# A filter in the frequency domain: first and last groups take another route through the engines

## The chip, the cores and the metric

The kernel runs on one core of one Trainium2 chip. A core has five engines with a queue of instructions each: TensorE (matmuls; PE in the profile), VectorE (DVE), ScalarE (ACT), GpSimd (POOL) and SyncE (SP), which here only issues transfers. The metric is the device time of one execution in microseconds; the median of several runs is compared.

## The reference, cut to what matters

Four layers alternate, each with a residual: layer A filters a layer-normed input in the two-dimensional frequency domain, and layer B is an attention over segments with a memory.

```python
def _A_ref(x, w_r, w_i):          # x: (1, 2048, 640)
    X = rfft2(x.astype(float32))  # 2048 x 321 complex
    X = X * (w_r + 1j * w_i)
    return irfft2(X, s=(2048, 640)).astype(bfloat16)

x = x + _A_ref(_layernorm(x), A_w_r, A_w_i)
x = x + _B_ref(_layernorm(x), ...)
x = x + _A_ref(_layernorm(x), A_w_r, A_w_i)
x = x + _B_ref(_layernorm(x), ...)
```

Only layer A is touched by the change; it occurs twice.

## The kernel before, in words

A layer A has three stages. The first multiplies the input by sine and cosine tables along part of the token axis and leaves `YT`. The second, `spectrum`, is what the change is about. The third, `tokens`, transforms back to rows (`psg`, L541, is its first matmul for each of 16 sets of rows; `psy`, L551 to L555, its second), adds the residual and computes the layer norm of layer B.

`spectrum` works through eight groups of frequencies, numbered j = 1, 2, 3, 4, 5, 6, 7, 0 in that order (`SEQ`). For each group it runs these steps:

- `along_d` (L420): two times ten matmuls of 321 columns transform the model axis, with cosines (o = 0, called ac) and with sines (o = 1, called db). ScalarE copies db to a buffer in SBUF, `dbs` (L428).
- `combine` (L432): VectorE writes the sum and the difference of ac and db as four bf16 rows, `P[j]` (L439, L440). Group 0 needs neither: its ac and db are only cast, one by VectorE (L437), one by ScalarE (L436).
- `across` (L442): for each of the two signs `sg`, four matmuls of `P[j]` against constants `K` finish the transform in two PSUM banks, `X`.
- `filt` (L453): for each sign, VectorE multiplies `X` by the real and by the imaginary filter values (L456): four products per group.
- `products` (L458): VectorE subtracts the products (L462), GpSimd adds them (L467; VectorE does that for groups 7 and 0), and GpSimd writes sum and difference of the two results as bf16, `sd[j]` (L469, L470). Before its addition GpSimd copies one element (`turn`, L466), which makes it wait for the subtraction. Group 0 needs no sum and difference.
- `back` (L472): for each of three chunks of the 321 columns (128, 128, 65), four matmuls of 256 columns (L488; L483 for group 0) begin the inverse transform in a PSUM bank, which ScalarE copies to `UT` (L490; VectorE for one chunk of group 0).

The order on TensorE, ScalarE, VectorE and GpSimd inside `spectrum` is the order of the text (`manual_schedule`, L493): the loop from L495 takes, for each i, the two transforms of group i, the steps across for group i - 1 and the way back of group i - 3, interleaved by hand. Every engine takes its own instructions strictly in that order. The PSUM pool of the stage has three pairs of banks with the tag `pg`, taken in turn by ac, db, X and one chunk of group 0, and two single banks with the tag `pu` for the other chunks of `back`. A step that takes a pair must wait until the reader of its last user is done. `SyncE` issues the filter rows of a later group after `products` (`load_w`, L514), and, gated by small ScalarE copies, the tables of the stage that follows and constants of layer B.

`BStart.begin` (L1480) reserves the transposed input of layer B; `BStart.memory` (L1501) clears the gaps in it with four memsets on GpSimd, during `tokens`.

Of the kernel before, what the change touches and what calls it, by code (L numbers as in the profile page):

```python
# [13 lines left out]
ALU = mybir.AluOpType  # L14
# [6 lines left out]
NF = 321  # L21
# [7 lines left out]
def _dft_tables():  # L29
# [22 lines left out]
    f = np.arange(321.0)  # L52
# [25 lines left out]
    for part in range(2):  # L78
        P = (1j if part else 1) * np.exp(1j * ps)
        for c in range(2):  # L80
            for k in range(8):
# [8 lines left out]
                for e, z in enumerate((se, de)):  # L90
                    M[c, part, e, :, k, :, q], M[c, part, e, :, k, :, r] = z.real, z.imag
    M = M.reshape(2, 2, 2, 128, 128)
    cK = np.stack([-kc, -ks, kc, ks] + [m for c in range(2) for m in (Kf[c].real, Kf[c].imag, -Kf[c].real)]
                  + [M[c, part, e] for c in range(2) for part in range(2) for e in range(2)], 1)
# [97 lines left out]
class LayerA:  # L192
# [8 lines left out]
    def tables(self, gate=None, mirror=True):  # L201
        nc, cd = self.tc.nc, self.g["cd"]
        s5 = self.ar.get("S5", f"{self.lname}tab")
        self.Fd = s5.bf(5, 2, NF)
        self.K = s5.bf(18, 128)
        self.Wm = s5.bf(2, 7 * NF)
        self.wts = [s5.bf(2, NF) for _ in range(3)]
        self.W = {}
        self.load_w(0)
        nc.sync.dma_start(out=self.Fd, in_=cd["cFd"])  # L210
        nc.sync.dma_start(out=self.K, in_=cd["cK"])
        self.load_w(1)
        self.load_w(2)
        for i in range(2 if mirror else 0):
            if gate is not None:
                _gate(nc, self.Wm[0:1, i, 0:1], gate)
            self.load_mirror(i)
# [175 lines left out]

    def spectrum(self, late_loads=()):
        tc, g, YT, Fd, K = self.tc, self.g, self.YT, self.Fd, self.K
# [5 lines left out]
        dbs = s1.f32(2, NF)  # L401
# [18 lines left out]
        def along_d(j, o):  # L420
            ab[j, o] = ps = pp.tile([128, 2, 512], FP32, name=f"ab{o}", tag="pg", bufs=3)
            for ch in range(5):
                for c in range(2):
                    nc.tensor.matmul(ps[:, 1 - c if o else c, 0:NF], lhsT=YT[:, ch, 2 * j + c, :, :].rearrange("p s k -> p (s k)"), rhs=Fd[:, ch, o, :],
                                     start=(ch == 0), stop=(ch == 4))
            if o == 1 and j:
                ab[j, o] = dbs
                nc.scalar.copy(out=dbs, in_=ps[:, :, 0:NF])  # L428

        pos = {j: p for p, j in enumerate(self.SEQ)}  # L430

        def combine(j):  # L432
            P[j] = quads[pos[j] % 2]
            ac, db = ab[j, 0], ab[j, 1]
            if j == 0:
                nc.scalar.copy(out=P[j][:, 2:4, :], in_=db[:, :, 0:NF])  # L436
                nc.vector.tensor_copy(out=P[j][:, 0:2, :], in_=ac[:, :, 0:NF])  # L437
                return
            nc.vector.tensor_tensor(out=P[j][:, 0:2, :], in0=ac[:, :, 0:NF], in1=db, op=ALU.add)  # L439
            nc.vector.tensor_tensor(out=P[j][:, 2:4, :], in0=ac[:, :, 0:NF], in1=db, op=ALU.subtract)  # L440

        def across(j, sg):  # L442
            X[j, sg] = x = pp.tile([128, 2, 512], FP32, name="X", tag="pg", bufs=3)
            if j == 0:
                a, b = (0, 3) if sg == 0 else (1, 2)
                k = 4 + 3 * sg
                ops = [(0, k, a), (0, k + 1, b), (1, k + 1, a), (1, k + 2, b)]
            else:
                ops = [(0, 2, 0), (0, 3, 3), (1, 2, 3), (1, 1, 0)] if sg == 0 else [(0, 2, 2), (0, 3, 1), (1, 0, 1), (1, 3, 2)]
            for i, (o, k, p) in enumerate(ops):  # L450
                nc.tensor.matmul(x[:, o, 0:NF], lhsT=K[:, k, :], rhs=P[j][:, p, :], start=(i % 2 == 0), stop=(i % 2 == 1))

        def filt(j, sg):  # L453
            x = X[j, sg]
            for t, xv, i in ((ts[pos[j] % 2][0], x[:, :, 0:NF], 0), (ts[pos[j] % 2][1], x[:, ::-1, 0:NF], 1)):
                nc.vector.tensor_tensor(out=t[:, sg, :, :], in0=xv, in1=W[j, sg][:, i, :].unsqueeze(1).to_broadcast([128, 2, NF]), op=ALU.mult)  # L456

        def products(j):  # L458
            sd[j] = quads[2 + pos[j] % 3]
            t1, t2 = ts[pos[j] % 2]  # L460
            a = sd[j].rearrange("p (c s) f -> p c s f", c=2) if j == 0 else acs[pos[j] % 2]
            nc.vector.tensor_tensor(out=a[:, 0, :, :], in0=t1[:, :, 0, :], in1=t2[:, :, 0, :], op=ALU.subtract)  # L462
            add = nc.vector
            if pos[j] < 6:
                add = nc.gpsimd
                add.tensor_copy(out=turn, in_=a[0:1, 0, 0, 0:1])  # L466
            add.tensor_tensor(out=a[:, 1, :, :], in0=t1[:, :, 1, :], in1=t2[:, :, 1, :], op=ALU.add)  # L467
            if j:
                nc.gpsimd.tensor_tensor(out=sd[j][:, 0:2, :], in0=a[:, :, 0, :], in1=a[:, :, 1, :], op=ALU.add)  # L469
                nc.gpsimd.tensor_tensor(out=sd[j][:, 2:4, :], in0=a[:, :, 0, :], in1=a[:, :, 1, :], op=ALU.subtract)  # L470

        def back(j, chunks):  # L472
            for ch in chunks:
                f0, f1 = CH[ch]
                m = f1 - f0
                if j == 0 and ch == 1:
                    psu = pp.tile([128, 2, 512], FP32, name="psu0", tag="pg", bufs=3)[:, 0, :].rearrange("p (e c k) -> p e c k", e=2, c=2)
                else:
                    psu = pp.tile([128, 2, 2, 128], FP32, name="psu2", tag="pu", bufs=2)
                if j == 0:  # L480
                    for c in range(2):
                        for part in range(2):
                            nc.tensor.matmul(psu[0:m, :, c, :], lhsT=sd[j][:, 2 * part + c, f0:f1], rhs=K[:, 10 + 4 * c + 2 * part:12 + 4 * c + 2 * part, :],  # L483
                                             start=(part == 0), stop=(part == 1))
                else:
                    for e, ops in enumerate((((0, 256), (3, 128)), ((1, 0), (2, 128)))):
                        for i, (o, k) in enumerate(ops):
                            nc.tensor.matmul(psu[0:m, e, :, :], lhsT=sd[j][:, o, f0:f1], rhs=Kf[:, k:k + 256], start=(i == 0), stop=(i == 1))  # L488
                for e in range(2):
                    (nc.vector.tensor_copy if j == 0 and ch == 1 else nc.scalar.copy)(out=UT[0:m, ch, e, :, j * 16:j * 16 + 16].rearrange("p s (c k) -> p s c k", c=2),  # L490
                                                                                in_=psu[0:m, e, :, :].rearrange("p c (s k) -> p s c k", k=8))

        with tc.manual_schedule(engines={nc.tensor.engine, nc.scalar.engine, nc.vector.engine, nc.gpsimd.engine}):  # L493
            rest = None
            for i in range(8 + 3):  # L495
                j, last, done = [self.SEQ[k] if 0 <= k < 8 else None for k in (i, i - 1, i - 3)]
                if j is not None:
                    along_d(j, 1)
                if rest is not None:
                    back(rest, (2,))  # L500
                    for _ in range(2):
                        if late:
                            late.pop(0)(UT[0:1, 0, 0, 0, rest * 16:rest * 16 + 1])
                if last is not None:
                    across(last, 0)
                    filt(last, 0)
                if j is not None:
                    along_d(j, 0)
                    combine(j)
                if last is not None:  # L510
                    across(last, 1)
                    filt(last, 1)
                    products(last)
                    if i + 2 < 8:  # L514
                        self.load_w(i + 2)
                rest = done
                if done is not None:
                    back(done, (0, 1))
            back(rest, (2,))
            for f in late:  # L520
                f(UT[0:1, 0, 0, 0, 112:113])

    def tokens(self, x_dst, xn_dst, handoff=None):
# [8 lines left out]
        pp = self.pp  # L532
        if handoff is not None:
            handoff.begin()

        def spectrum_d(s0):
# [935 lines left out]
class BStart:  # L1472
# [7 lines left out]
    def begin(self):  # L1480
        self.hT = self.ar.get("S2", f"{self.lname}hT").bf(5, self.st.NK + 12)

    def wv_piece(self, i):
# [17 lines left out]
    def memory(self, pp):  # L1501
        nc = self.tc.nc
        for a, b in self.st.hgap:
            nc.gpsimd.memset(self.hT[:, :, a:b], 0.0)
        psm = pp.tile([128, 5, 128], BF16, name="psm0", tag="pu", bufs=2)
# [170 lines left out]
def kernel(  # L1676
# [26 lines left out]
    a1.cold(A_x[0])  # L1703
    a1.spectrum(late_consts(tc, g))
    a1.tokens(x1[:], n1[:], b1)
    layer_B(tc, g, ar, b1, x1[:], None, f1, a2)
    a2.spectrum()
    a2.tokens(x3[:], n3[:], b2)
# [49 lines left out]
```

## Time and profile before

| what | time |
|---|---|
| median of 5 runs | 1566.17 us (1565.74 to 1567.28) |
| the profiled execution's own time | 1567.24 us |
| its span, from the first to the last instruction | 1565.40 us |
| first spectrum stage, first L424 to first L541 | 26.50 to 76.79 us |
| second spectrum stage, first L424 to first L541 | 795.43 to 845.41 us |
| mean granted clock of TensorE | 0.997 of full speed |

Instruction rows give start, duration, engine, line, operation, output and inputs with their shapes, a count where several are merged, and in brackets the idle time of the engine before the row with what ended it. Durations overlap their successors by a little[...]; the step from one start to the next is the rate.

### The profile page before, as it was taken

Reading aid. Unit: us, or ns where it says so; the run is one execution under the profiler, and the core shown is the slowest. Engines: PE = TensorE matmul, PEld = TensorE weight load, DVE = VectorE, ACT = ScalarE, POOL = GpSimd, SP = SyncE. Lnnn points to the kernel's source line nnn. Section 1 sums busy time; section 2 is a strip of 40 time slices with the busy share of each in tenths; the row PEclk is TensorE's granted clock in tenths of the full one; section 3 lists DMA queues with packets and bytes.
Section 4 is the critical chain, followed back from the end, with each engine's and each line's share of the span. In section 5 each row is a group of like instructions: output and inputs, shape, how many; then the busy total and the mean of one; then the engine's idle time right before and its main releaser. Section 6 shows DMA issues by size and latency. Waiting matters only on the chain. (4 is left out here: it accounts for less than half of the span.)

```text
span 1565.4 us, 36413 instructions
## 1 busy us (share of the span) xinstructions
PE 1531.0 (98%) x14418; PEld 1073.5 (69%) x14419; DVE 816.9 (52%) x2438; ACT 768.9 (49%) x2245; POOL 238.5 (15%) x329
## 2 busy tenths in 40 slices
PE   7999999999999999999999999999999999999998
PEld 6676666666666666677766766666666666667775
DVE  7872545565456555633377635565456555553111
ACT  4484565555555565511126655556555565562000
POOL 3620021111111121100034101111111121110000
PEclk9999999999999999999999999999999999999999
DMA  4681334334443443636114614434443435427242
GB/s 170 206 298 44 115 132 157 137 124 149 148 141 137 141 131 149 197 104 179 51 48 140 199 38 155 137 126 146 150 140 137 146 126 176 126 99 229 68 128 64
DMA packets 159764, 214.79 MB, mean 137 GB/s; under 512 B 7136, under 2 KB 133096, under 8 KB 151648
## 3 DMA queue, kind: packets, MB, share of 16 engines
q1 hardware_dynamic: 159008, 210.08, 40.9%
q8 instruction: 114, 1.87, 0.5%
q0 software_dynamic: 576, 2.30, 0.4%
q14 instruction: 66, 0.54, 0.1%
HBM read 167.26 MB, written 45.10 MB: 136 GB/s over the span
## 5 line engine op out<-in xcount | busy, mean ns | idle before, releaser
L1087 PEld LDWEIGHTS <-bB_S 128*128 128x128 bf16 x3180 | 261.3, 97 | 179.8 <-issue 0.6
L1146 DVE CAST bB_S<-psk 128x495 bf16<-128x495 f32 (+3 forms) x320 | 191.6, 599 | 277.0 <-PE psk L1087 272.3
L1429 PE MATMUL psx<-Wo_sb,bB_S 128*128 128x320 bf16 x2048 | 287.7, 299 | 0.1
L1166 ACT ACTIVATE bB_S<-pss 128x269 bf16<-128x269 f32 (+5 forms) x576 | 208.9, 387 | 138.5 <-PE pss L1163 138.2
L1429 PEld LDWEIGHTS <-bB_S 128*128 128x128 bf16 x2048 | 196.7, 98 | 74.7 <-DVE bB_S L1250 0.7
L1131 ACT ACTIVATE bB_S<-psq 128x96 bf16<-128x96 f32 x300 | 152.1, 507 | 173.3 <-PE psq L1087 173.3
L1206 POOL TENSOR_TENSOR bB_S<-bB_S,bB_S 128x535 f32<-128x535 f32 x90 | 111.6, 1253 | 819.7 <-DVE bB_S L1198 762.3
L1250 DVE TENSOR_TENSOR bB_S<-pso,bB_S 128x480 bf16<-128x480 f32 (+1 forms) x320 | 192.7, 603 | 74.0 <-DMA bB_S<-Rd 52.0
L1167 DVE TENSOR_TENSOR bB_S<-bB_S,maskf 128x269 bf16<-128x269 bf16 (+5 forms) x576 | 158.8, 289 | 112.4 <-ACT bB_S L1166 112.4
L1155 ACT CAST bB_S<-psv 128x512 bf16<-128x512 f32 (+1 forms) x288 | 162.4, 564 | 80.9 <-PE psv L1153 80.9
L1153 PE MATMUL psv<-bB_S,B1hT_S 128*128 128x256 bf16 x1360 | 168.8, 273 | 0.0
L1153 PE MATMUL psv<-bB_S,B2hT_S 128*128 128x256 bf16 x1360 | 168.8, 273 | 0.0
L1087 PE MATMUL psk<-B1hT_S,bB_S 128*128 128x495 bf16 (+3 forms) x800 | 164.3, 343 | 0.2 <-ACT bB_S L1108 0.2
L1087 PE MATMUL psk<-B2hT_S,bB_S 128*128 128x495 bf16 (+3 forms) x800 | 164.3, 343 | 0.2 <-ACT bB_S L1108 0.2
L1087 PE MATMUL psq<-B1hT_S,bB_S 128*128 128x495 bf16 (+5 forms) x780 | 156.0, 337 | 0.0
L1087 PE MATMUL psq<-B2hT_S,bB_S 128*128 128x495 bf16 (+5 forms) x780 | 156.0, 337 | 0.0
L1153 PEld LDWEIGHTS <-B1hT_S 128*128 128x128 bf16 x1360 | 129.9, 98 | 24.3
L1153 PEld LDWEIGHTS <-B2hT_S 128*128 128x128 bf16 x1360 | 129.9, 98 | 24.3
L1163 PE MATMUL pss<-bB_S 128*128 128x132 bf16 (+8 forms) x1152 | 137.7, 219 | 0.0
L1163 PEld LDWEIGHTS <-bB_S 128*128 128x128 bf16 x1152 | 95.5, 98 | 55.3
L1236 PE MATMUL pso<-bB_S,bB_S 128*128 128x132 bf16 (+8 forms) x1152 | 118.7, 219 | 2.1 <-DVE oTmf L1253 1.4
L1236 PEld LDWEIGHTS <-bB_S 128*128 128x128 bf16 x1152 | 89.1, 98 | 34.7 <-DVE oTmf L1253 2.8
(283 smaller groups left out, 1427.9 us busy)
## 6 DMA issues: line engine op xcount, KB each, us to landing
bB_S<-Rd SPq DMA_DIRECT2D x62, 1070.0 KB
oTx_d<-bB_S SPq DMA_DIRECT2D x60, 512.0 KB
bB_S<-oTx_d SPq DMA_DIRECT2D x46, 512.0 KB
bB_S<-in_B_Wq_dram SPq DMA_DIRECT2D x32, 320.0 KB
bB_S<-in_B_Wk_dram SPq DMA_DIRECT2D x32, 320.0 KB
bB_S<-in_B_Wv_dram SPq DMA_DIRECT2D x32, 320.0 KB
Wo_sb<-in_B_Wo_dram SPq DMA_DIRECT2D x4, 1280.0 KB
B1wv_S<-in_B_Wv_dram SPq DMA_DIRECT2D x10, 512.0 KB
```

The costliest lines, as they stand in the source:

```text
L1087: nc.tensor.matmul(ps, lhsT=w[:, ch, hh * 128:(hh + 1) * 128], rhs=src[:, ch, lo:hi], start=(ch == 0), stop=(ch == 4))
L1131: nc.scalar.mul(out=qv[:, :, 0:SEG], in_=x_view(ps, o, n)[:, :, 1:SW], mul=scale)
L1146: nc.vector.tensor_copy(out=KTs[h % 2][:, lo:hi], in_=ps[:, 0:hi - lo])
L1153: nc.tensor.matmul(ps[:, i * 256:(i + 1) * 256], lhsT=hT[:, ch, st.hcol((t + i) * 128):st.hcol((t + i) * 128) + 128], rhs=w["Wv"][:, ch, : ...
L1155: nc.scalar.copy(out=V[:, t:t + n, :].rearrange("p a b -> p (a b)"), in_=ps[:, 0:n * 256])
L1163: nc.tensor.matmul(ps[:, off - o0:off - o0 + hi - lo], lhsT=KT[:, t * 128:(t + 1) * 128], rhs=QT[:, lo:hi], start=True, stop=True)
L1166: nc.scalar.activation(out=E[:, 0:n], in_=ps[:, 0:n], func=ACTF.Exp)
L1167: nc.vector.tensor_tensor(out=P[:, o0:o0 + n], in0=E[:, 0:n], in1=bs.mask[:, o0:o0 + n], op=ALU.mult)
L1206: nc.gpsimd.tensor_tensor(out=acc, in0=acc, in1=part, op=ALU.add)
L1236: nc.tensor.matmul(pso[:, lo - q0:hi - q0], lhsT=V[:, t, (h % 2) * 128:(h % 2 + 1) * 128], rhs=P[:, off:off + hi - lo], start=(i == 0), st ...
L1250: nc.vector.tensor_tensor(out=oT.rearrange("p (r s j) -> p r s j", r=16, j=2)[:, :, s0:s0 + ns, :], in0=byclass(po), in1=rx, op=ALU.mult)
L1429: self.tc.nc.tensor.matmul(ps[:, 0:320], lhsT=lhs(h, k // 2), rhs=self.g["Wo_sb"][:, h, c0:c0 + 320], start=(h == 0), stop=(h == H - 1))
```

## The change

- The first group's ac and db (j = 1) go to `P[j]` as bf16 by two ScalarE copies, without sum and difference. `across` then takes eight matmuls for each sign instead of four, with the signs in the constants; `K` gets one more matrix (-kc, now 19). Group 0's cast of ac moves from VectorE to ScalarE.
- For groups 6 and 7 (`SPLIT`) `products` writes the difference (VectorE) and the sum (GpSimd) of the filter products straight to `sd[j]` as bf16. `back` takes eight matmuls per chunk instead of four, four on each half, so that no sum and difference on GpSimd is needed. Group 7's halves are ordered so that its two first chunks use the first half before the second.
- The first filter product of group 0 goes to GpSimd, after a ScalarE copy of X from PSUM to `dbs`.
- Group 0's subtraction and addition are each cut in two pieces of 128 and 193 columns.
- The last chunk of groups 6 and 7 takes a spare pair of banks (`pg`); the chunks of one call get their banks first and are copied out after all of them have been multiplied.
- The order is written out anew: group 1 goes across for both signs before group 2 is transformed; group 7's `products` come after group 0's first sign.
- The four memsets move from `memory` to `begin`, which is now called at the end of `spectrum`.

```diff
-    cK = np.stack([-kc, -ks, kc, ks] + [m for c in range(2) for m in (Kf[c].real, Kf[c].imag, -Kf[c].real)]
+    cK = np.stack([-kc, -ks, kc, ks, -kc] + [m for c in range(2) for m in (Kf[c].real, Kf[c].imag, -Kf[c].real)]
...
-            if o == 1 and j:
+            if o == 1:
+                P[j] = quads[pos[j] % 2]
                 ab[j, o] = dbs
-                nc.scalar.copy(out=dbs, in_=ps[:, :, 0:NF])
+                nc.scalar.copy(out=P[j][:, 2:4, :] if j in RAW else dbs, in_=ps[:, :, 0:NF])
...
+        Q = self.SEQ
+        RAW, SPLIT = (Q[0], 0), Q[5:7]
...
-            if j == 0:
-                nc.scalar.copy(out=P[j][:, 2:4, :], in_=db[:, :, 0:NF])
-                nc.vector.tensor_copy(out=P[j][:, 0:2, :], in_=ac[:, :, 0:NF])
+            if j in RAW:
+                nc.scalar.copy(out=P[j][:, 0:2, :], in_=ac[:, :, 0:NF])
                 return
...
+            elif j in RAW:
+                ops = ([(0, 2, 2), (0, 1, 3), (1, 1, 2), (1, 0, 3), (0, 2, 0), (0, 3, 1), (1, 2, 1), (1, 1, 0)] if sg == 0 else
+                       [(0, 0, 2), (0, 3, 3), (1, 1, 2), (1, 0, 3), (0, 2, 0), (0, 3, 1), (1, 0, 1), (1, 3, 0)])
...
+                mul = nc.vector
+                if j == 0 and sg == 0 and i == 0:
+                    nc.scalar.copy(out=dbs, in_=xv)
+                    mul, xv = nc.gpsimd, dbs
+                mul.tensor_tensor(out=t[:, sg, :, :], in0=xv, in1=W[j, sg][:, i, :].unsqueeze(1).to_broadcast([128, 2, NF]), op=ALU.mult)
...
+            a = sd[j].rearrange("p (c s) f -> p c s f", c=2) if j == 0 or j in SPLIT else acs[pos[j] % 2]
+            for f0, f1 in ((0, 128), (128, NF)) if j == 0 else ((0, NF),):
+                nc.vector.tensor_tensor(out=a[:, 0, :, f0:f1], in0=t1[:, :, 0, f0:f1], in1=t2[:, :, 0, f0:f1], op=ALU.subtract)
+                add = nc.vector
+                if j:
+                    add = nc.gpsimd
+                    add.tensor_copy(out=turn, in_=a[0:1, 0, 0, 0:1])
+                add.tensor_tensor(out=a[:, 1, :, f0:f1], in0=t1[:, :, 1, f0:f1], in1=t2[:, :, 1, f0:f1], op=ALU.add)
+            if j and j not in SPLIT:
...
+                if ch == (1 if j == 0 else 2) and pos[j] > 4:
...
+            for ch, m, psu in outs:
+                inverse(j, ch, m, psu, 0)
+                if j == Q[5]:
+                    inverse(j, ch, m, psu, 1)
+            for ch, m, psu in outs if j == Q[6] else ():
+                inverse(j, ch, m, psu, 1)
...
+            elif j in SPLIT:
+                for e, ks in enumerate(((256, 256), (128, 384)) if part == 0 else ((128, 384), (0, 0))):
+                    for s, k in enumerate(ks):
+                        nc.tensor.matmul(psu[0:m, e, :, :], lhsT=sd[j][:, 2 * part + s, f0:f1], rhs=Kf[:, k:k + 256], start=(part + e + s == 0),
+                                         stop=(part + s == 2), skip_group_check=True)
...
+            def gate(p, sg):
+                across(Q[p], sg)
+                filt(Q[p], sg)
+                if sg and p != 6:
+                    products(Q[p])
+                    if p < 5:
+                        self.load_w(p + 3)
...
+            first_half(0)
+            second_half(0)
+            gate(0, 0)
+            gate(0, 1)
+            first_half(1)
+            second_half(1)
+            for p in range(2, 8):
+                first_half(p)
+                if p >= 4:
+                    rest(p - 4)
+                gate(p - 1, 0)
+                second_half(p)
+                gate(p - 1, 1)
+                if p >= 3:
+                    back(Q[p - 3], (0, 1))
+            gate(7, 0)
+            products(Q[6])
+            rest(4)
+            gate(7, 1)
+            for p in range(5, 8):
+                back(Q[p], (0, 1))
+                rest(p)
...
+            if handoff is not None:
+                handoff.begin()
```

Here `first_half` is `along_d` with sines, `second_half` is `along_d` with cosines and `combine`, and `rest` is `back` for chunk 2 with the gated loads.

## The prediction

> **What bounds the kernel now.** I read the page first, then its 40 slices, then stretches of the time line by stage.
>
> ```profile
> PE 1531.0 (98%) x14418; PEld 1073.5 (69%) x14419; DVE 816.9 (52%) x2438; ACT 768.9 (49%) x2245; POOL 238.5 (15%) x329
> ```
>
> TensorE (PE) is busy nearly everywhere, so only stretches in which it waits can give time back without taking matmuls away. The table of busy time by stretch shows where: the two spectrum stages.
>
> ```profile
> 24.80:74.00 49.20, 43.68 (x329) 30.60 (x326) 44.46 (x60) 18.74 (x58) 28.74 (x30) 0.99 0.51 167
> 110.00:795.20 685.20, 681.55 (x6499) 476.16 (x6499) 345.76 (x1112) 337.90 (x1021) 79.33 (x78) 1.00 0.40 131
> 795.20:843.00 47.80, 42.90 (x306) 29.83 (x307) 43.78 (x62) 17.34 (x51) 28.73 (x30) 0.98 0.19 54
> ```
>
> The columns are the stretch, its length, the busy time of PE, PE's weight loads, VectorE (DVE), ScalarE (ACT) and GpSimd (POOL), PE's clock, the DMA share, GB/s. In a spectrum stage VectorE is busy for 44 of 48 us, as long as PE. The middle groups repeat every 5.33 us, with PE back to back and VectorE full. The tail is different (time line of PE; the bracket is PE's idle time and its releaser):
>
> ```profile
> 835.41 1.26 PE L451 MATMUL X<-A2tmp_S,A2tab_S 128*128 128x321 bf16 x8
> 836.51 0.27 PE L488 MATMUL psu<-A2tab_S,A2tmp_S 128*128 128x256 bf16 x1
> 837.09 0.94 PE L488 MATMUL psu<-A2tab_S,A2tmp_S 128*128 128x256 bf16 x7 [0.31 <-POOL A2tmp_S L470]
> 838.33 0.60 PE L488 MATMUL psu<-A2tab_S,A2tmp_S 128*65 128x256 bf16 x4 [0.30 <-ACT A2UT_S L490]
> 839.91 0.28 PE L488 MATMUL psu<-A2tab_S,A2tmp_S 128*128 128x256 bf16 x1 [0.99 <-POOL A2tmp_S L469]
> 841.19 2.56 PE L488 MATMUL psu<-A2tab_S,A2tmp_S 128*128 128x256 bf16 x11 [0.99 <-POOL A2tmp_S L470]
> 843.59 1.99 PE L483 MATMUL psu<-A2tab_S,A2tmp_S 128*128 128x256 bf16 x12
> 845.41 2.04 PE L541 MATMUL psg<-A2gt_S,A2UT_S 128*128 128x321 bf16 x12
> ```
>
> From 836.5 on PE waits for GpSimd's sums and differences (L469, L470), which wait for VectorE. And the waiting slows PE itself; by single microseconds the columns are length, PE busy, clock, DMA share, GB/s:
>
> ```profile
> 840.00:841.00 1.00, 0.20 (x1) 1.00 0.00 0
> 841.00:842.00 1.00, 0.81 (x4) 0.62 0.00 0
> 842.00:843.00 1.00, 1.00 (x7) 0.50 0.00 0
> 843.00:844.00 1.00, 1.00 (x7) 0.50 0.00 0
> 844.00:845.00 1.00, 1.00 (x8) 0.67 0.00 0
> ```
>
> The clock halves for 3.3 us after the stretch with little work. The first stage shows the same at 73.4 to 76.7. VectorE and GpSimd in the tail:
>
> ```profile
> 835.71 1.32 POOL L470 TENSOR_TENSOR A2tmp_S<-A2gt_S 128x642 bf16<-128x642 f32 x1
> 836.38 1.34 DVE L462 TENSOR_TENSOR A2gt_S<-A2tmp_S 128x642 f32<-128x642 f32 x1
> 837.64 0.82 DVE L467 TENSOR_TENSOR A2gt_S<-A2tmp_S 128x642 f32<-128x642 f32 x1
> 838.54 1.32 POOL L469 TENSOR_TENSOR A2tmp_S<-A2gt_S 128x642 bf16<-128x642 f32 x1 [1.08 <-DVE A2gt_S L467]
> 842.17 0.82 DVE L467 TENSOR_TENSOR A2tmp_S<-A2tmp_S 128x642 bf16<-128x642 f32 x1
> ```
>
> L462 takes 0.83 us in six of seven groups and 1.34 here, beside L470.
>
> **Durations used**, start to start: a matmul of 321 columns 0.137 us (ten in 1.37), of 256 columns 0.122 (eight in 0.97 to 1.04; 0.11 in the 65-row chunk); a 642-element VectorE operation 0.735, its result usable 0.87 after its start; a ScalarE copy 0.59, usable at 0.74; GpSimd 1.28 with bf16 output (lasting 1.32), 1.55 with fp32; last matmul's start to its reader 0.39 (321 columns) or 0.31 (256). With each engine in its program order these reproduce the stage before: L462 at 836.38 as in the trace, the first L541 at 844.7 against 845.41 (0.7 or so is the halved clock).
>
> **The change part by part, per stage.** Groups run 1 to 7, then 0.
>
> PE gains work: group 1 across s: 8 more matmuls, 1.10 us. Groups 6 and 7 back: 12 more each, 24 in all, 16 x 0.122 + 8 x 0.11 = 2.83. Together 3.9 us, all on the engine that already bounds the middle.
>
> VectorE loses five operations: the add and subtract of group 1, the cast of group 0 (L437), one filter product of group 0, the addition of group 7 (L467): 5 x 0.735 = 3.7 us; cutting group 0's two products in four adds about 0.14 (256 and 386 elements at the rate of 642, plus the fixed part: 2 x 0.335 + 2 x 0.47 = 1.61 against 1.47). Net 3.5 us. GpSimd loses four sums and differences (5.1 us) and gains an addition and a product. ScalarE gains about three copies of 0.59; it is busy 17 of 48 us, so only the copy in the start is on the path. New waits on it: the copy of group 0's X waits for PE, and behind it stand the evictions of group 5's last chunk, which nobody needs before the L541.
>
> *Start.* PE does its 20 matmuls from 795.43 to 798.17 as before. Then group 1's two differences-by-PE: four matmuls on the second copy at once, the other four when ScalarE has cast the first half: 798.42 + 0.74 = 799.16, a stall of 0.45. The last of the eight starts at 799.57, VectorE's first filter product at 799.96 (before 800.64, but with two operations already done). Four products: 802.9; the subtraction; group 2's add and subtract at 803.79 and 804.52; PE waits for the latter until 805.39; group 2's first filter product at 806.06. Before it stood at 805.92. So the start is worth nothing: VectorE saves 1.47 us there and idles for as much. -0.1.
>
> *Middle.* Unchanged to the group: 5.32 us of PE against 5.3 of VectorE.
>
> *Tail.* PE has group 0's first four matmuls at 834.73, group 5's last chunk 835.28, group 0's other four 835.72 to 836.27; then group 6: 2.83 us to 839.10, group 7's first halves 0.98 to 840.08, a wait, its second halves with the last chunk 1.86, group 0's twelve 1.42. Beside it ScalarE copies group 0's X at 835.63, GpSimd multiplies 836.37 to 837.92, VectorE subtracts for group 7 (held until then: 838.66), filters to 840.13, makes group 0's four pieces 840.26 to 841.8. GpSimd adds for group 7 at 839.02 (after its one-element copy), lasting to 840.34, so PE waits 0.33 and goes on at 840.40; 842.26 group 0 begins, its inputs ready; the first L541 comes at 843.74. Before: 845.41. PE's stalls in the tail fall from 4.3 us to 0.4, and its clock should stay up.
>
> The first pair of L541 rounds keeps 0.33 us of waits for evictions of UT: L551 at 845.65 against 847.29 in the trace, **-1.64 us**. In the first stage (the same layout 768.93 earlier) 76.72 against 78.66, **-1.94**, since its slow-clock stretch lay worse. Sum **-3.58 us**. What follows is bound by PE and issues its loads relative to it, so the gain is carried to the end.
>
> *Without cost.* The constants' transfer grows from 576 to 608 KB, 0.1 us at 370 GB/s; it is issued at 6.38 and was in by 17.7, PE wants it at 29; without that cover it would delay the start by 0.1. The four memsets (0.49 us, in GpSimd's wait at 836.97 before) now stand behind its last addition; its next work is at 852. If that cover were gone, a layer norm would be 0.5 late. The filter loads keep their place after each group's products on the SP queue; the Wv pieces that wait on that queue for the temporary buffer's release move with the tail. The eviction banks: chunk 2 of groups 6 and 7 takes a spare pair, which removes the 0.30 waits (L490).
>
> **Two rules.** Rows: L462 at 1.34 beside L470, ending about 0.7 after it. The Trainium skill, "SBUF — State Buffer", section "SBUF: two separate sides", says that VectorE operations with two SBUF inputs and GpSimd exclude each other for a whole instruction. This speaks against the new GpSimd product, which begins within 0.1 us of group 7's subtraction. With the exclusion L541 is at 843.74, without it at 843.3; I keep the first.
> Clock: the rows show half speed after 3.4 us in which PE was busy for about 40%. "TensorE: Matmul & The Clock Gate", Part 1, asks for an idle window of about 3.4 us. By its letter the tail before would not have slowed; the row decides. In the new tail PE idles 0.4 of 9 us, so by both there is no slowing. If it came all the same, 3.3 us at half speed would cost up to 1.6 a stage.
>
> **Not shown before.** The GpSimd product (fp32 with a broadcast bf16 factor): nearest the fp32 L467, 1.55; lower end the bf16-output 1.32 (-0.2 a stage), upper end twice the row, 3.1 (+1.5 a stage). The j=0 matmuls (L483) appear at half clock mostly; 0.122 taken, 0.2 at most, +0.9 a stage.
>
> **Rivals.**
> A, likeliest, 0.60: as summed, 1562.6, own range 1561.5 to 1563.4.
> B, the relief is half hidden, 0.20: the tail stays with VectorE and GpSimd through the exclusion, or the clock still drops; a gain of 0.9 a stage, 1566.2 - 1.8 = 1564.4. For it: PE gets 3.9 us of work in the stage it bounds. Against: the stalls are 4.3 us there.
> C, more, 0.15: the start keeps VectorE's 1.4 us of slack and passes it down in both stages: 1566.2 - 3.6 - 2 = 1560.6. Against it: PE alone fills 5.32 of 5.33.
> D, slower, 0.05: the GpSimd product is slow. It delays group 7's subtraction, then its addition and PE, one for one; at 3.2 us (1.55 + 1.67) the gain is gone in the second stage, at 5 us the kernel stands at about 1562.6 + 2 x 3.45 = 1569.5. Against: all twelve fp32 rows lie at 1.53 to 1.56.
> That the edit does nothing is excluded: matmul counts change.
>
> **How the numbers follow.** The profiled execution took 1567.24 around a span of 1565.40; the sum predicts a span of 1561.8. The median of the runs is 1566.17; less 3.58: 1562.6. 0.2%, what a measurement of this kernel can tell, is 3.1 us. 0.50 of A's 0.60 and all of C's 0.15 are past it: faster 0.65; B, the rest of A and the mild end of D (0.01): same 0.31; the rest of D: slower 0.04. Range 1560.5 (C) to 1564.9 (B's upper part).
>
> **What would show it.** Right: L541 starts at about 74.8 and 843.7; clock 1.00 throughout; idle before L488 in the tail below 1 us; group 2's first filter product at about 806. Wrong: a GpSimd product over 2 us, a clock of 0.5 in 838 to 845, VectorE's subtraction for group 7 over 2 us with PE waiting for it, or the second group's filter well before 805.5 (C).

## The result, and the profile after

The changed kernel takes 1562.94 us in the median against 1566.58 for the kernel before, a ratio of 0.9978 with a 95% interval of 0.9972 to 0.9983: 3.6 us less, where 3.58 were forecast. The total is right. The terms that make it up are not all right, and their errors cancel by luck; the experiments below take them apart.

In the changed file the lines have moved: `across` is L455, the filter products L464, the subtraction L471, the addition L476, GpSimd's sums L478 and L479, the way back L516 for plain groups, L511 for groups 6 and 7, L506 for group 0, the copies to UT L498, the first matmul of the stage that follows (psg) L582 and its second (psy) L592.

The first line is from the page of the changed kernel; the others are its busy time by stretch (length, busy PE, PE's weight loads, VectorE, ScalarE, GpSimd, then clock, DMA share, GB/s), the second spectrum stage taken where it now lies:

```profile
PE 1532.9 (98%) x14482; PEld 1078.6 (69%) x14483; DVE 809.7 (52%) x2432; ACT 772.5 (49%) x2251; POOL 234.5 (15%) x327
...
24.80:74.00 49.20, 47.57 (x375) 35.37 (x372) 41.67 (x59) 21.96 (x66) 26.59 (x29) 1.00 0.52 167
...
794.40:842.00 47.60, 46.49 (x354) 34.22 (x353) 40.66 (x56) 21.38 (x60) 26.61 (x29) 1.00 0.19 54
```

PE was busy for 43.7 of the first 49.2 us and is now for 47.6, although the stage in it has become shorter; VectorE has fallen from 44.5 to 41.7. The roles are those of the forecast: PE took work over and fills the stage. The stage itself is shorter than forecast: its first psg comes 47.31 us after its first matmul (840.97 - 793.66), where the forecast had 48.31 (843.74 - 795.43).

The tail of the second stage on PE:

```profile
833.27 0.71 PE L455 MATMUL X<-A2tmp_S,A2tab_S 128*128 128x321 bf16 x4
833.82 3.68 PE L511 MATMUL psu<-A2tab_S,A2tmp_S 128*128 128x256 bf16 x32
837.87 1.93 PE L511 MATMUL psu<-A2tab_S,A2tmp_S 128*128 128x256 bf16 x16 [0.37 <-POOL A2tmp_S L476]
839.64 1.49 PE L506 MATMUL psu<-A2tab_S,A2tmp_S 128*128 128x256 bf16 x12
840.97 2.04 PE L582 MATMUL psg<-A2gt_S,A2UT_S 128*128 128x321 bf16 x12
```

One wait of 0.37 us is left, where 0.33 was forecast, for the same reason: GpSimd's addition for group 7. The clock stays up in the last microseconds (columns as above):

```profile
839.00:840.00 1.00, 1.00 (x12) 0.95 (x10) 0.38 (x1) 0.88 (x4) 0.00 (x0) 1.00 0.00 0
840.00:841.00 1.00, 1.00 (x12) 0.90 (x9) 0.28 (x1) 1.00 (x4) 0.00 (x0) 1.00 0.00 0
```

VectorE and GpSimd beside it:

```profile
833.98 1.41 POOL L464 TENSOR_TENSOR A2tmp_S<-A2tmp_S,A2tab_S 128x642 f32<-128x642 f32 x1 [1.36 <-issue]
834.68 1.40 DVE L471 TENSOR_TENSOR A2tmp_S<-A2tmp_S 128x642 bf16<-128x642 f32 x1
836.27 1.54 POOL L476 TENSOR_TENSOR A2tmp_S<-A2tmp_S 128x642 bf16<-128x642 f32 x1
838.83 0.55 DVE L476 TENSOR_TENSOR A2tmp_S<-A2tmp_S 128x386 bf16<-128x386 f32 x1
```

The new GpSimd product takes 1.41 us, and the subtraction beside it 1.40 instead of 0.83.

**Stage by stage.** From each trace I take four lengths: from a stage's first L424 to the first psy (stage 1 and stage 2), from the first psy to the second stage's first L424 (between), and from the second psy to the end (rest). They are the measure of all that follows: the medians scatter by about 1 us, the stage of the changed kernel by 0.02 (after and e10). The two stretches outside the stages scatter by more.

| kernel | stage 1 | stage 2 | between | rest | median, ratio to before, interval |
|---|---|---|---|---|---|
| before | 52.16 | 51.86 | 716.76 | 718.14 | |
| e9, before again | 51.85 | 50.76 | 716.78 | 717.96 | 1567.54, 1.0000, 0.9991 to 1.0008 |
| e11, memsets only | 50.87 | 50.83 | 716.79 | 717.84 | 1566.04, 0.9998, 0.9990 to 1.0007 |
| e5, before with filling | 50.80 | 50.77 | 718.60 | 718.07 | 1566.54, 0.9994, 0.9986 to 1.0002 |
| after | 49.19 | 49.18 | 718.03 | 718.56 | 1562.94, 0.9978, 0.9972 to 0.9983 |
| e10, after again | 49.18 | 49.18 | 717.75 | 718.31 | 1563.32, 0.9980, 0.9972 to 0.9988 |
| e1, product on VectorE | 49.19 | 49.17 | 717.16 | 718.76 | 1563.76, 0.9978, 0.9971 to 0.9986 |
| e2, sums on GpSimd again | 54.25 | 54.41 | 716.78 | 718.61 | 1574.44, 1.0043, 1.0029 to 1.0057 |
| e3, group 1 as before | 49.12 | 49.10 | 717.67 | 718.05 | 1562.66, 0.9967, 0.9955 to 0.9979 |
| e4, no spare banks | 49.65 | 49.64 | 717.29 | 718.72 | 1564.07, 0.9979, 0.9970 to 0.9989 |
| e6, one piece | 49.18 | 49.18 | 718.45 | 718.51 | 1562.81, 0.9967, 0.9954 to 0.9981 |
| e12, three edits undone | 49.11 | 49.08 | 717.65 | 718.16 | 1562.31, 0.9973, 0.9963 to 0.9984 |
| e7, ten matmuls more | 50.35 | 50.34 | 718.63 | 718.42 | 1566.20, 0.9994, 0.9986 to 1.0002 |
| e8, thirty more | 53.08 | 53.07 | 718.99 | 718.02 | 1571.48, 1.0025, 1.0015 to 1.0035 |

The kernels ran in groups of four, each against the kernel before on the same chip (its medians there: 1567.45, 1567.27, 1566.78); ratios are comparable across groups, medians only within one.

In the two profiles compared first, the stages lost 2.97 and 2.68 us, 5.65 in sum, and the span only 4.0, the medians only 3.6. My theory at that point: the tail was freed as forecast, and layer B gives part of it back. The rival: the difference lies in the profiles themselves, that is, one execution of each kernel doesn't stand for all.

### The profile page after: what moved, and what is told of

Its sections match the earlier page's. It is cut to its first block, busy times and chain, and to the rows that moved or that the text cites. A ratio compares the mean times of both kernels' runs of the same rounds, so it can differ in the third digit from the quotient of the medians.

```text
span 1561.4 us, 36535 instructions
## 1 busy us (share of the span) xinstructions
PE 1532.9 (98%) x14482; PEld 1078.6 (69%) x14483; DVE 809.7 (52%) x2432; ACT 772.5 (49%) x2251; POOL 234.5 (15%) x327
## 3 DMA queue, kind: packets, MB, share of 16 engines
q8 instruction: 115, 1.88, 0.5%
```

## The experiments

**Group 0's product back on VectorE (e1).**

```diff
-                if j == 0 and sg == 0 and i == 0:
-                    nc.scalar.copy(out=dbs, in_=xv)
-                    mul, xv = nc.gpsimd, dbs
```

> The changed kernel with group 0's first filter product back on VectorE, without the ScalarE copy. Exclusion theory: the GpSimd product holds up VectorE's subtraction for group 7 by about 0.6 us (it lasts 1.40 us instead of 0.83), so moving 0.735 us away from VectorE frees only 0.15; each stage gets 0.1 to 0.2 us longer, about 1563.2 us in all. Rival, the product is simply off VectorE: 0.7 us a stage, about 1564.4 us. In the profile: group 7's subtraction back at 0.83 us under the first theory.

The stages did not move at all (49.19, 49.17), less even than the first theory's 0.1 to 0.2. VectorE and GpSimd in the first stage's tail:

```profile
68.65 0.82 DVE L468 TENSOR_TENSOR A1tmp_S<-A1tmp_S 128x642 bf16<-128x642 f32 x1
...
69.74 1.54 POOL L473 TENSOR_TENSOR A1tmp_S<-A1tmp_S 128x642 bf16<-128x642 f32 x1
```

The subtraction takes 0.82 again. With the product on GpSimd it starts 0.51 us earlier (41.02 us after the stage's first matmul, 834.68 - 793.66, against 41.53, 68.65 - 27.12), but it lasts 0.58 longer. So GpSimd's addition begins at the same time, 42.6 us after the first matmul in both kernels (69.74 - 27.12, 836.27 - 793.66). That VectorE is held up beside GpSimd eats the product's whole gain; the rival is out.

**Sums for groups 6 and 7 on GpSimd again (e2).**

```diff
-        RAW, SPLIT = (Q[0], 0), Q[5:7]
+        RAW, SPLIT = (Q[0], 0), ()
```

(with the two conditions on `Q[5]` and `Q[6]` in `back` made to follow it.)

> The changed kernel with sums and differences for groups 6 and 7 on GpSimd again (24 matmuls fewer a stage). Tail theory: GpSimd's sum and difference for group 7 come only 2.6 us after its addition, PE waits, and each stage gets 1.8 to 2.8 us longer; with what layer B gives back, 1565.5 to 1568 us, so most of the gain is gone, and the clock may halve in the tail again. Rival, the 24 matmuls cost as much as they save: no change, 1562.9 us or less.

5.1 and 5.2 us a stage, twice the expected, and slower than the kernel before. First PE's waits in the first stage, then VectorE and GpSimd:

```profile
68.94 1.38 PE L516 MATMUL psu<-A1tab_S,A1tmp_S 128*128 128x256 bf16 x11 [1.00 <-POOL A1tmp_S L479]
73.97 0.39 PE L516 MATMUL psu<-A1tab_S,A1tmp_S 128*128 128x256 bf16 x1 [3.65 <-POOL A1tmp_S L478]
75.43 0.82 PE L516 MATMUL psu<-A1tab_S,A1tmp_S 128*128 128x256 bf16 x3 [1.07 <-POOL A1tmp_S L479]
```

```profile
71.14 1.59 DVE L471 TENSOR_TENSOR A1tmp_S<-A1tmp_S 128x256 bf16<-128x256 f32 x1
72.66 1.54 DVE L476 TENSOR_TENSOR A1tmp_S<-A1tmp_S 128x256 bf16<-128x256 f32 x1
74.11 1.68 DVE L471 TENSOR_TENSOR A1tmp_S<-A1tmp_S 128x386 bf16<-128x386 f32 x1
75.72 0.55 DVE L476 TENSOR_TENSOR A1tmp_S<-A1tmp_S 128x386 bf16<-128x386 f32 x1
68.85 1.99 POOL L464 TENSOR_TENSOR A1tmp_S<-A1tmp_S,A1tab_S 128x642 f32<-128x642 f32 x1
...
70.92 1.53 POOL L476 TENSOR_TENSOR A1gt_S<-A1tmp_S 128x642 f32<-128x642 f32 x1
72.52 1.39 POOL L478 TENSOR_TENSOR A1tmp_S<-A1gt_S 128x642 bf16<-128x642 f32 x1
73.87 1.50 POOL L479 TENSOR_TENSOR A1tmp_S<-A1gt_S 128x642 bf16<-128x642 f32 x1
```

GpSimd's product, addition, sum and difference follow each other without a break. Of group 0's four pieces on VectorE, 0.41 to 0.55 us each in the changed kernel, three take 1.5 to 1.7 here, and each of these ends 0.3 to 0.4 after the end of a GpSimd operation. PE stands for 3.65 us at once, and the clock goes to 0.5. I had counted GpSimd's chain and left out what it does to VectorE. This run measures the splitting together with an order that is made for it, so it doesn't give the splitting's worth against the kernel before. It shows that the rest of the change depends on the 24 extra matmuls a stage: without them it is a loss.

**Group 1 as before (e3).**

```diff
-        RAW, SPLIT = (Q[0], 0), Q[5:7]
+        RAW, SPLIT = (0,), Q[5:7]
...
-            gate(0, 0)
-            gate(0, 1)
             first_half(1)
+            gate(0, 0)
             second_half(1)
+            gate(0, 1)
```

> The changed kernel with group 1 as before: VectorE's sum and difference, eight matmuls fewer a stage, the old order in the start. Layout theory: the start is worth nothing either way, group 2's first filter product stands 10.5 us after the stage's first matmul in both; 1562.9 us within 0.5. Rival, VectorE bounds the stage from its first operation on: 1.5 us a stage longer, about 1565 us.

0.07 and 0.08 us shorter a stage: the start is worth nothing. In the changed kernel group 2's first filter product stands 10.58 us after the stage's first matmul (804.24 - 793.66), before it was 10.49.

**Without the spare banks (e4).**

```diff
-                if ch == (1 if j == 0 else 2) and pos[j] > 4:
+                if j == 0 and ch == 1:
```

> The changed kernel with the last chunk of groups 6 and 7 in the two single banks again. Layout theory: group 6 waits about 0.15 us for the eviction of its first chunk, group 7 0.3; 0.3 to 0.6 us a stage, 1563.4 to 1564 us. Rival, the chunks of eight matmuls (0.9 us) cover ScalarE's two copies (0.6 us) and the banks are free in time: no change.

0.46 a stage, within the expected 0.3 to 0.6, but not with the expected waits. PE in the first stage:

```profile
71.52 1.56 PE L511 MATMUL psu<-A1tab_S,A1tmp_S 128*128 128x256 bf16 x12 [0.29 <-ACT A1UT_S L498]
73.38 1.04 PE L511 MATMUL psu<-A1tab_S,A1tmp_S 128*65 128x256 bf16 x8 [0.30 <-ACT A1UT_S L498]
```

Both waits are in group 7: its second chunk waits for the copy of group 6's last, and its last chunk for the copy of its own first. Group 6 waits for nothing, where 0.15 was expected, and the 0.37 for GpSimd's addition falls away behind the first wait. The ratio alone, 0.9979, would not have told this run from the changed kernel.

**The kernel before with PE kept busy (e5).** In `back`, for group 7's first chunk, ahead of each of its first two matmuls:

```diff
+                            if j == Q[6] and ch == 0 and e == 0:
+                                for _ in range(8):
+                                    nc.tensor.matmul(psu[0:m, 1, :, :], lhsT=K[:, 0, :], rhs=Kf[:, 0:256], start=(i == 0), stop=True, skip_group_check=True)
```

> The kernel before with 16 extra matmuls of 256 columns a stage, whose results are overwritten: eight ahead of group 7's first chunk and eight between its first two matmuls, where PE waits for GpSimd 0.99 us each time. Clock theory: PE stays at full speed in the tail, the last 23 matmuls run at 0.11 instead of 0.2 us, and each stage gets 0.7 to 1.2 us shorter though PE does 1.8 us more work; 1564.3 to 1565.3 us. Rival, the tail's length is VectorE's and GpSimd's alone and PE's clock is hidden, or the extra matmuls push the others back: 1566.6 us or more.

In the stages the clock theory holds: 1.36 and 1.09 us shorter than in the first profile of before, although PE does 1.8 us more (16 matmuls of 0.11). PE alone, by microsecond, in the first stage (length, busy PE, clock, DMA share, GB/s):

```profile
71.00:72.00 1.00, 1.00 (x9) 1.00 1.07 364
72.00:73.00 1.00, 1.00 (x10) 1.00 1.06 361
73.00:74.00 1.00, 0.88 (x9) 1.00 1.07 365
74.00:75.00 1.00, 0.70 (x7) 1.00 0.69 230
```

Yet the medians show 0.7 us with an interval that holds zero, not 2.4. In this profile the stretch between the stages is 1.8 us longer than in that of before, which could hide most of it; or the kernel before doesn't lose 2.4 us to its clock in every execution. That led to the runs of the third group.

**Before again (e9) and after again (e10).** Neither has an edit.

> The kernel before, unchanged, against itself. The two profiles so far give stages shorter by 5.7 us in sum and a program shorter by 3.6 in the medians. If the difference is the executions' own scatter between the stages, this run's time from the first stage's end to the second's start lies as high as in the others (717 to 719 us, against 716.8 in the profile shown) and its ratio is 1.000. If it is the kernel before that has shorter stretches between the stages, 716.8 comes again.

> The changed kernel, unchanged, on the chip of the other three. Scatter theory: the stages at 49.2 us as before, the stretch between them anywhere in 717 to 719 us, a ratio of 0.9978 within 0.0007. If the stages' gain is carried whole: 0.9964.

The changed kernel repeats its stages to 0.01 us. The kernel before doesn't: in one execution its first stage takes 51.85 and its second 50.76. PE's clock in the two tails of e9 and at the end of its program, in stretches of 3.41 us (columns as in the fence above):

```profile
68.42:71.83 3.41, 1.16 (x8) 1.00 1.07 362
71.84:75.25 3.41, 3.39 (x16) 0.50 0.43 147
...
836.42:839.83 3.41, 1.78 (x12) 1.00 0.00 0
839.84:843.25 3.41, 2.48 (x20) 1.00 0.00 0
...
1560.05:1563.40 3.35, 0.00 (x0) 0.50 0.03 10
```

The instructions are the same, with waits of the same lengths; the first tail ends with the clock halved, the second doesn't. What differs is how the stretches lie. Within a program the clock is halved for 3.41 us, or for twice that (e2). In the three traces with more than one fall of the clock, the falls of a trace lie on one grid, whose step is 3.4133 us (768.00 / 225):

| trace | the clock falls at (us) | from one to the next | in steps |
|---|---|---|---|
| before | 73.24, 841.24, 1561.45 | 768.00, 720.21 | 225, 211 |
| e9 | 71.84, 1560.05 | 1488.21 | 436 |
| e2 | 71.82, 843.23, 1570.27 | 771.41, 727.04 | 226, 213 |

The stretches in the fence above are steps of e9's grid. In its first tail one step holds most of the waits, with PE busy for 1.16 us, and the next step runs at half speed; in the second tail the same waits are shared by two steps, with 1.78 and 2.48 us of work. The first profile of before fits:

```profile
69.82:73.23 3.41, 1.43 (x10) 1.00 1.07 362
73.24:76.65 3.41, 3.12 (x15) 0.50 0.15 51
...
837.82:841.23 3.41, 1.13 (x8) 1.00 0.00 0
841.24:844.65 3.41, 3.41 (x17) 0.50 0.00 0
```

The rows of PE in e9:

```profile
71.86 2.57 PE L488 MATMUL psu<-A1tab_S,A1tmp_S 128*128 128x256 bf16 x11 [0.99 <-POOL A1tmp_S L470]
74.27 1.95 PE L483 MATMUL psu<-A1tab_S,A1tmp_S 128*128 128x256 bf16 x12
...
842.26 1.49 PE L483 MATMUL psu<-A2tab_S,A2tmp_S 128*128 128x256 bf16 x12
```

Group 0's twelve matmuls take 1.79 us to the next row where the clock is low and 1.34 (to 843.60) where it isn't. So the kernel before has stages of 50.8 us without and 51.85 to 52.16 with the halving; the profile I worked from had it in both.

How often it comes can be read from the mean clock of PE, which is on record for every execution. The first profile of before, with both tails halved, has 0.997, e9, with one, 0.998, e11 below, with none, 0.999; a halving takes 0.5 x 3.41 us from about 1565, that is 0.0011. Of the 107 executions of the kernel before in the three groups 43 have 0.997 or less, 47 have 0.998 and 17 have 0.999. All 42 of the changed kernel (its first runs and e10) have 0.999 or 1.000. So 1.2 of the two tails are halved in an average execution, 0.6 a stage. That is an estimate, since the fall at the program's end takes another 0.0002 to 0.0013 off the mean in these traces. The times go with it: on e9's chip the executions of the kernel before took 1565.4 us on average at 0.999, 1566.3 at 0.998 and 1567.6 below.

The stretch between the stages was 716.8 again; the scatter theory's 717 to 719 did not come for the kernel before. e10's ratio is 0.998, as the scatter theory had it.

**The memsets alone (e11).** The four memsets and the reservation moved to the end of `spectrum` in the kernel before.

```diff
     def begin(self):
         self.hT = self.ar.get("S2", f"{self.lname}hT").bf(5, self.st.NK + 12)
+        for a, b in self.st.hgap:
+            self.tc.nc.gpsimd.memset(self.hT[:, :, a:b], 0.0)
...
             for f in late:
                 f(UT[0:1, 0, 0, 0, 112:113])
+            if handoff is not None:
+                handoff.begin()
```

> The kernel before with one edit of the change alone: the four memsets and the reservation of layer B's input at the end of the spectrum stage. Cover theory: stages 52.16 and 51.86 us as before, no change in time, 1.000. If any other program than the one before has longer stretches between the stages (as all eight so far had by 1 to 2.3 us in the medians), this one too: 1.0007 to 1.0015.

0.9998: no change, as expected. Its stages are 50.87 and 50.83, not the expected 52: this execution escaped the halving twice. On its grid, counted back from the fall at 1558.68, the waits of each tail are shared by two steps (in the second tail with 1.75 and 2.12 us of work). The first tail:

```profile
67.05:70.46 3.41, 1.88 (x14) 1.00 1.06 361
70.47:73.88 3.41, 1.97 (x14) 1.00 0.84 285
```

It is not the memsets that shorten them, since e9's second stage and both of e5's have the same length without that edit.

**Group 0's results in one piece (e6).**

```diff
-            for f0, f1 in ((0, 128), (128, NF)) if j == 0 else ((0, NF),):
+            for f0, f1 in ((0, NF),):
```

> The changed kernel with group 0's subtraction and addition in one piece each. Theory: PE reaches group 0's first matmul (839.64) later than either form needs; no change, 1562.9 us within 0.5. Rival, the first chunk waits for the whole pair: 0.3 to 0.5 us a stage longer.

49.18 in both stages, to the hundredth: PE reaches group 0 later than either form.

**Three edits undone at once (e12)**: e1, e3 and e6 together.

> The changed kernel with three of its edits undone at once: group 1 as before, group 0's product on VectorE, its subtraction and addition in one piece. What stays: groups 6 and 7 without sums on GpSimd, the spare banks, the order of the tail, group 0's cast on ScalarE. From the single runs: e3 -0.08 us a stage, the others 0.00 to 0.02; stages of 49.1 to 49.3 us, the time of the changed kernel within its interval. If the edits stand in for each other, so that one alone was not missed: 0.5 to 1.5 us a stage longer.

49.11 and 49.08: they don't stand in for each other. The splitting without the spare banks, the new order of the tail and group 0's cast on ScalarE was not run. The simpler version is at least as fast: 1562.31 against 1563.32 for the changed kernel in the same group, with overlapping intervals, so I call it equal in time and not better.

**Ten and thirty matmuls more at the end of each stage (e7, e8).**

```diff
+            psf = pp.tile([128, 2, 512], FP32, name="psf", tag="pg", bufs=3)
+            for i in range(10):
+                nc.tensor.matmul(psf[:, i % 2, 0:NF], lhsT=K[:, 0, :], rhs=Fd[:, 0, 0, :], start=True, stop=True)
```

> The changed kernel with ten matmuls more (1.37 us) at the end of each spectrum stage, whose results nobody reads. If what follows the stages keeps a shift whole: 2.5 to 2.7 us longer, about 1565.5 us. If layer B takes up a part of any shift (from before to after the stages lost 5.6 us and the program 3.6, a slope of 0.65): 1.6 to 1.8 us longer, about 1564.6 us.

> The same with thirty matmuls more (4.1 us) at the end of each stage, 8.2 us in all. Shift kept whole: 8.0 us longer, about 1570.9 us. Slope of 0.65: 5.3 us longer, about 1568.2 us. If layer B's loss hangs on chance alignment and not on the size of the shift, the slopes of this run and of the one with ten differ from each other and lie on both sides of 1.

To the first psy the stages grew by 1.16 (e7) and 3.89 us (e8), so 2.3 and 7.8 in sum. Against the median difference of the changed kernel (-3.64), those of e7 (-1.07) and e8 (+4.21) are 2.6 and 7.85 us higher. A shift is kept whole; layer B takes up no fixed share of it, and that theory falls.

## Why the prediction was right, and where it was not

- **The bound and the tail: right.** The one wait left is the forecast one, 0.37 us, and e2 shows what carries it. The 4.3 us of stalls that the forecast gives to the tail before were read too high: the waits in its rows add up to 2.6 (0.31 + 0.30 + 0.99 + 0.99).
- **The start at nothing: right**, 10.58 against 10.49 us, and e3.
- **PE's own gain: right in mechanism, too small.** Against the kernel before at full clock (50.8) the stage gained 1.6 us. My sum had about 0.9: 1.64, less the 0.7 or so that I gave to the clock. Three terms were mis-sized. First, the middle was put as unchanged. Yet two of PE's waits for VectorE's filter products, 0.73 and 0.39 us, are gone, and PE begins the cosine half of group 0 35.83 us after the stage's first matmul (829.49 - 793.66), where it was 36.30 (831.73 - 795.43). Two rows before, one after:

```profile
807.53 1.55 PE L424 MATMUL ab<-A2tab_S,A2YT_S 128*128 128x321 bf16 x10 [0.73 <-DVE A2tmp_S L456]
831.73 1.53 PE L424 MATMUL ab<-A2tab_S,A2YT_S 128*128 128x321 bf16 x10 [0.39 <-DVE A2tmp_S L456]
...
829.49 1.53 PE L424 MATMUL ab<-A2tab_S,A2YT_S 128*128 128x321 bf16 x10
```

Second, GpSimd's addition for group 7, which ends PE's wait, comes 42.61 us after the first matmul instead of 43.59 (839.02 - 795.43): the GpSimd product begins 0.62 us earlier than in my layout, takes 1.41 instead of 1.55 and holds up the subtraction less. The addition then takes 1.54 instead of 1.32. Third, a matmul of 256 columns was put at 0.122 us; the 16 from 837.87 to 839.64 run at 0.11.

- **The clock: the step that failed.** I read the halving off one execution and took it for a property of the kernel in both stages. It comes only where a step of the grid holds enough of the waits: in three of the six stages profiled without an edit to their timing (before, e9, e11), and by the mean clocks in about 0.6 of all. When it comes it costs 1.05 to 1.4 us, so about 0.7 a stage on average, where I had charged 0.7 and 1.0 in every execution. The 0.7 itself was a remainder of my replay of the stage, which stood too high: 49.27 us to the first psg (844.7 - 795.43), where e9's second stage, at full clock, has 48.89 (843.60 - 794.71). The reading of the rule was right in one point: a wholly idle window isn't needed. It was wrong in taking the row as what decides for every execution. In the tail after, with PE idle for 0.4 us, no stage of after, e1, e3, e6, e10 or e12 slowed, as forecast.
- **"Carried to the end": right** by e7 and e8, for a shift. Still, with 1.6 from the order of work and about 0.7 on average from the clock, two stages should give 4.6 us, and the medians give 3.5 to 3.6. About 1.0 is given back outside the stages: between them before, e9 and e11 have 716.8 us, the changed kernel 718.03 and 717.75, the other kernels 716.78 to 718.99; the rest is 717.84 to 718.14 in the first three and 718.31 and 718.56 in the changed kernel. Where it is lost is seen: in the changed kernel PE waits 1.03 us at 624.35 for VectorE's scaling of the attention output, at the same place before 0.27, and 0.34 in the first matmuls of layer B under "issue"; in e10 these are 0.22 and 0.88. Why it is lost more often there is open; no run tells it. The time at which the stage ends can't be the whole cause: in e7 and e11 the first psy stands at 76.89 us, and the stretch after it takes 718.63 and 716.79.
- **Without cost: right** for the memsets (e11) and the pieces (e6). The pieces, group 1's route and the GpSimd product are not only without cost, but without use (e6, e3, e1, and all three in e12).
- **The rivals.** D, a slow GpSimd product, did not come: 1.41 us. B, half of the relief hidden by the exclusion, holds for the product alone (e1), not for the stage. C, a gain in the start, is out.

So 3.58 forecast and 3.64 measured agree by luck: the order of work brought 3.2 us instead of 1.9, the clock about 1.4 instead of 1.7, and the 1.0 or so that is given back outside the stages stood in no term.

## What to carry to other kernels

Where a matrix unit waits for sums that a slower engine makes only to feed it, the sum can be left to the matrix unit's accumulator; the gain is the wait, and here it counted at the end of a stage, where nothing else filled it. Before a part of a gain is put down to the clock, look whether a second execution shows the same, and how the mean clock spreads over all of them. A stage whose length is repeatable to 0.02 us is a better yardstick than a median with 1 us of scatter. Moving an operation from VectorE to GpSimd beside a two-input VectorE operation can bring nothing: here that operation took 1.40 us instead of 0.82, and the gain was gone.

## What was not expected of the hardware

The clock halved or didn't after the same instructions and the same waits. What decides in these traces is how a grid of 3.41 us, which runs through the whole program, lies against them: a step with PE busy for 1.13, 1.16 or 1.43 us is followed by one at half speed, steps with 1.78 (e9) or 1.88 (e11) aren't. So one profile can't tell whether a kernel pays. The Trainium skill, "TensorE: Matmul & The Clock Gate", Part 1, calls the activity window free-running, of about 3.4 us; the grid of the falls agrees with that. And GpSimd's hold on VectorE chains up: in e2 three pieces in a row each waited for the next GpSimd operation and took three to four times their time.
